# Batch 0's first kv products ahead of the second transposes, and two x products of batches 1 and 2 moved, in an attention-and-GEGLU kernel

## Chip, cores and metric

One core of a Trainium2 chip. The metric is the device time of one execution in microseconds (us), median of several runs. The profiled span is about 1.8 us shorter than the time of the same run and is used for places within the kernel.

## The reference

```python
q_s = softmax(q, axis=-1)              # over the head dimension, 64
k_s = softmax(k, axis=2)               # over the sequence, 576
kv  = einsum('bhsd,bhse->bhde', k_s, v)
x   = einsum('bhsd,bhde->bhse', q_s, kv)    # 8 batches, 8 heads
x   = x.transpose(0, 2, 1, 3).reshape(4608, 512)
out = (gelu(x @ w_gate) * (x @ w_val)) @ w_out   # d_ff = 1536
```

Of the kernel before, what the change touches and what calls it, by code (L numbers as in the profile page):

```python
# [18 lines left out]
def kernel(  # L19
# [17 lines left out]
    NFI = F // P  # L37
# [56 lines left out]
    wg_sb = wpool.tile([P, HP, F], f16, name="wg_sb")  # L94
    wv_sb = wpool.tile([P, HP, F], f16, name="wv_sb")
# [28 lines left out]
    def copy_on(eng, dst, src):  # L124
        if eng == "pool":
            nc.gpsimd.tensor_copy(out=dst, in_=src)  # L126
        elif eng == "act":
            nc.scalar.copy(out=dst, in_=src)  # L128
        else:
            nc.vector.tensor_copy(out=dst, in_=src)  # L130

    def cast_w(nm, c, eng="pool"):
        dst = (wg_sb if nm == "wg" else wv_sb)[:, :, WCH[c]:WCH[c + 1]]
        copy_on(eng, dst, wst[(nm, c)])
# [18 lines left out]
    def cast_v(b, h0, h1, eng="pool"):  # L153
        if eng == "pool" and h1 - h0 > 2:
            for h in range(h0, h1, 2):
                cast_v(b, h, h + 2)
            return
        copy_on(eng, v16_b[b % 2][:, :, h0:h1, 0:D].rearrange("p n h d -> p h n d"),
                tiles[("v", b)][:, h0:h1, :].rearrange("p h (n d) -> p h n d", d=D))
# [44 lines left out]
    st = {}  # L204

    def kv_mm(b, g, j):
        if (b, "pskv", g) not in st:
            pool, tag = (ps_big, "mm") if (b, g) == (0, 1) else (ps_att, "att")
            st[(b, "pskv", g)] = pool.tile([P, 2, 2 * VW], f32, name="pskv", tag=tag)
        hp = 2 * g + j  # L210
        for n in range(NC):
            nc.tensor.matmul(  # L212
                st[(b, "pskv", g)][:, j, :], ek_b[b % 2][:, n, hp * P:(hp + 1) * P],
                v16_b[b % 2][:, n, 2 * hp:2 * hp + 2, 0:VW],
                start=(n == 0), stop=(n == NC - 1))

    def kv_norm(b, g):
        pskv = st[(b, "pskv", g)]
        rck = att.tile([P, 2], f32, name="rck", tag="rck")
        nc.vector.reciprocal(out=rck, in_=pskv[:, :, D])  # L220
        for j in range(2):
            kv_sb = att.tile([P, 2, D], f16, name="kv_sb", tag="kv", bufs=12)
            nc.vector.scalar_tensor_tensor(  # L223
                out=kv_sb,
                in0=pskv[:, j, :].rearrange("p (h e) -> p h e", e=VW)[:, :, 0:D],
                scalar=rck[:, j:j + 1], in1=mask, op0=ALU.mult, op1=ALU.mult)
            st[(b, "kv", 2 * g + j)] = kv_sb
# [6 lines left out]
    def get_eqt(b):  # L234
        if (b, "eqt") not in st:
            st[(b, "eqt")] = att.tile([P, HP * 4 * NC * 32], f16, name="eqt", tag="eqt")[
                :, 0:HP * S].rearrange("p (h t) -> p h t", h=HP)
        return st[(b, "eqt")]

    def unit_t(b, g, eng="dve"):  # L240
        eqt = get_eqt(b)
        pst = ps_att.tile([P, 2, MAIN], f16, name="pst", tag="att")
        for j in range(2):
            hp = 2 * g + j
            for n in range(NM):
                nc.tensor.transpose(  # L246
                    pst[:, j, n * P:(n + 1) * P],
                    eq_b[b % 2][:, n + 1, hp * P:(hp + 1) * P], ident)
        st["evac_t"] = lambda eng: copy_on(eng, eqt[:, 2 * g:2 * g + 2, 0:MAIN], pst)
        if eng:  # L250
            st["evac_t"](eng)
# [66 lines left out]
    def warm_pe(n):  # L318
        ps = pswarm
        for _ in range(n):  # L320
            nc.tensor.matmul(ps, ident, warm, start=True, stop=True)  # L321
# [5 lines left out]
    def mm_gv(ps, w, xt, fi, cis):  # L327
        for ci in cis:
            nc.tensor.matmul(ps, w[:, ci, fi * P:(fi + 1) * P], xt[:, ci, :],  # L329
                             start=(ci == 0), stop=(ci == HP - 1))  # L330

    def gate(psg, psv):
        gl = ffn.tile([P, 512], f32, name="gl", tag="gl")
        nc.scalar.activation(out=gl, in_=psg, func=ACTF.Gelu)  # L334
        ht = htp.tile([P, 512], f16, name="ht", tag="ht")
        nc.vector.scalar_tensor_tensor(  # L336
            out=ht, in0=psv, scalar=_H_SCALE, in1=gl, op0=ALU.mult, op1=ALU.mult)
        return ht
# [5 lines left out]
        mm_gv(psv, wv_sb, xt, fi, range(HP))  # L344
        return gate(psg, psv)

    def ffn_first(xt, after):

        ps = []
        for fi in range(len(after)):  # L350
            psg = ps_big.tile([P, 512], f32, name="psg", tag="mm")
            mm_gv(psg, wg_sb, xt, fi, range(0, 2))
            psv = ps_big.tile([P, 512], f32, name="psv", tag="mm")
            mm_gv(psv, wv_sb, xt, fi, range(0, 2))
            ps.append((psg, psv))
            for f in after[fi]:
                f()
        for fi, (psg, psv) in enumerate(ps):
            mm_gv(psg, wg_sb, xt, fi, [2])
            mm_gv(psv, wv_sb, xt, fi, [2])  # L360
        hts = []
        for fi, (psg, psv) in enumerate(ps):
            mm_gv(psg, wg_sb, xt, fi, [3])
            mm_gv(psv, wv_sb, xt, fi, [3])
            hts.append(gate(psg, psv))
        return hts

    def ffn_first0(xt, xs):

        ps = {}  # L370
        for fi in range(2):
            for nm in ("g", "v"):
                ps[(nm, fi)] = ps_big.tile([P, 512], f32, name="ps" + nm, tag="mm")

        def go(fi, cis):
            for ci in cis:
                mm_gv(ps[("g", fi)], wg_sb, xt, fi, [ci])
                mm_gv(ps[("v", fi)], wv_sb, xt, fi, [ci])

        go(0, (0, 1))  # L380
        xs()
        go(1, (0, 1))
        go(0, (2,))
        go(1, (2,))
        hts = []
        for fi in range(2):
            go(fi, (3,))
            hts.append(gate(ps[("g", fi)], ps[("v", fi)]))
        return hts
# [85 lines left out]
    evac_t0 = st["evac_t"]  # L475
    norm_pair(0, 1, 1, ("dve", "pool"))
    evac_t0("dve")
    warm_pe(9)
    unit_t(0, 1, None)
    cast_v(0, 0, 2, "dve")  # L480
    cast_v(0, 2, 4, "act")
    cast_v(0, 6, 8, "dve")
    cast_v(0, 4, 6, "act")
    st["evac_t"]("act")
    for h0 in (0, 4):
        load(k, "k", 1, h0, h0 + 4, 0)
        load(v, "v", 1, h0, h0 + 4, 0)
    load_batch(2, ((q, "q"), (k, "k")))
    nc.sync.dma_start(out=q0r, in_=q[0].rearrange("h (m n) d -> m h (n d)", n=NT)[:, :, 0:D])
    warm_pe(1)  # L490
    kv_mm(0, 0, 0)
    kv_mm(0, 0, 1)
    kv_norm(0, 0)
    kv_mm(0, 1, 1)
    cast_w("wg", 0, "pool")
    cast_w("wv", 0, "pool")
# [12 lines left out]
    FI, NS = 0, 1  # L509
    plan = {}  # L510

    def at(b, kind, i, *fns):
        plan.setdefault((b, kind, i), []).extend(fns)

    L = lambda f, *a: (lambda: f(*a))
# [7 lines left out]
    at(0, NS, 6, L(norm, 1, 3))  # L523
    at(0, NS, 17, L(unit_x, 1, 0, "act", True), L(unit_x, 1, 1, "act", True))
    at(0, NS, 7, L(preload, ACTF.Gelu))
    first1 = [[L(unit_kv, 1, 1), L(unit_t, 1, 1)], [L(unit_x, 1, 2, "act")],
              [L(unit_x, 1, 3, "dve")]]

    def x_upper():
        unit_x(0, 2, "dve")  # L530
# [13 lines left out]
    at(1, NS, 1, L(unit_x, 2, 0, "dve"))  # L544
    at(1, NS, 12, L(unit_kv, 2, 1))
    at(1, NS, 2, L(unit_x, 2, 1, "dve"), L(unit_x, 2, 2, "dve"))
    at(1, NS, 3, L(unit_x, 2, 3, "act"))
    at(2, FI, 0, L(unit_xrem, 2, "dve"))
    at(2, FI, 7, L(norm_rem0))
    at(3, FI, 8, L(unit_trem, 0))  # L550
# [32 lines left out]
    def ride(b, kind, i):  # L583
        for fn in plan.get((b, kind, i), []):
            fn()

    for b in order:
        xt = get_xt(b) if b < B else xtr
        hts = []
        fi0 = 0  # L590
        if b < 2:
            hts = ffn_first0(xt, x_upper) if b == 0 else ffn_first(xt, first1)
            fi0 = len(hts)
            ride(b, FI, fi0 - 1)
        for fi in range(fi0, NFI):
            hts.append(ffn_fi(xt, fi))
            ride(b, FI, fi)
        if b == 0:
            psys = []
            for ns in range(4):  # L600
                psys.append(ps_big.tile([P, C], f32, name="psy", tag="mm"))
                mm_out(psys[ns], hts, ns, range(0, NFI // 2))
                ride(b, NS, ns)
            for ns in range(4):
                cut = 9 if ns == 3 else NFI
                mm_out(psys[ns], hts, ns, range(NFI // 2, cut))
                ride(b, NS, 14 + ns)
                mm_out(psys[ns], hts, ns, range(cut, NFI))
                evac(b, ns, psys[ns], "act" if ns == 3 else "dve")
                ride(b, NS, 4 + ns)  # L610
        else:
            for ns in range(4):
                if b == order[-1] and ns == 3:
                    last_rows(b, hts, ns)
                    break
                psy = ps_big.tile([P, C], f32, name="psy", tag="mm")
                mm_out(psy, hts, ns, range(NFI // 2))
                ride(b, NS, 10 + ns)
                mm_out(psy, hts, ns, range(NFI // 2, NFI))
                evac(b, ns, psy)  # L620
                ride(b, NS, ns)
# [30 lines left out]
```

## The kernel before: what the change touches

The work is cut by batch. For a batch, q is normalised (`norm`), transposed 128x128 at a time into a PSUM tile `pst` (`unit_t`) that is then copied to `eqt` (the evacuation); `kv_mm` gives `pskv` for two head pairs, `kv_norm` scales it into `kv_sb`; `unit_x` multiplies both into `psx`, which is cast into a row `xt[:, hp]` (four rows per batch, one for each head pair). A gate tile (`fi`) adds four such rows (`ci`) into `psg` and into `psv`. `psxr` is the x product of the rows that are left over when 576 is cut into 128s. `psy` is the output product. The schedule is written by hand: TensorE takes its instructions in the order of this code.

```python
# start, batch 0
    norm_pair(0, 1, 1, ("dve", "pool"))
    evac_t0("dve")
    warm_pe(9)                     # matmuls without use, to fill the wait
    unit_t(0, 1, None)             # second transposes
    cast_v(0, 0, 2, "dve"); cast_v(0, 2, 4, "act")
    cast_v(0, 6, 8, "dve"); cast_v(0, 4, 6, "act")
    st["evac_t"]("act")            # ScalarE copies them out of PSUM
    ...                            # (loads cut)
    warm_pe(1)
    kv_mm(0, 0, 0); kv_mm(0, 0, 1)
    kv_norm(0, 0)
    kv_mm(0, 1, 1)
    ...
    unit_x(0, 0, "act", True)      # then kv_mm(0, 1, 0), unit_x(0, 1), first gate matmul
# batch 1's first three gate tiles
    def ffn_first(xt, after):
        for fi in range(len(after)):
            psg = ...; mm_gv(psg, wg_sb, xt, fi, range(0, 2))
            psv = ...; mm_gv(psv, wv_sb, xt, fi, range(0, 2))
            for f in after[fi]: f()
        ...                        # then row 2 of all three, then row 3
    first1 = [[L(unit_kv, 1, 1), L(unit_t, 1, 1)], [L(unit_x, 1, 2, "act")],
              [L(unit_x, 1, 3, "dve")]]
# what rides behind what; NS 10..13: amid an output tile, NS 0..3: behind it
    at(1, FI, 7, L(exp, "k", 2, 0, 4), L(cast_v, 2, 0, H))
    at(1, FI, 11, L(load_batch, 3), ..., L(cast_v, 3, 0, H))
    at(1, NS, 3, L(unit_x, 2, 3, "act"))
    ...                            # batch 0's last output tile:
    cut = 9 if ns == 3 else NFI    # the x products of batch 1 go behind the cut
```

The softmax here doesn't subtract the row's maximum and nothing guards it: scores larger than these inputs give would overflow.

## Time and profile before

| | before |
|---|---|
| time, median of the first 3 runs | 320.91 us (320.80 to 320.92) |
| span of the profiled run | 319.1 us |
| TensorE busy | 312.4 us, 98% |
| VectorE, ScalarE, GpSimd busy | 193.8, 140.6, 45.2 us |
| TensorE's waits in its own list | six short ones, all before 88 us |

How the gaps between matmuls are counted (from start to start, with a step of 0.216 us at 512 columns), and the lines themselves, are in the prediction.

### The profile page before, as it was taken

How to read it: one execution, taken by the hardware profiler on the slowest of the kernel's cores; microseconds unless marked ns; L12 is line 12 of the kernel's file. 1: busy time of each engine (PE TensorE's matmuls, PEld its weight loads, DVE VectorE, ACT ScalarE, POOL GpSimd, SP SyncE). 2: the span in 40 equal slices, each digit the busy share in tenths (PEclk: the TensorE clock that was granted, in tenths of full speed). 3: DMA queues.
4: the chain of work that ended last, by engine and by line, in shares of the span. 5: the costliest groups of instructions: out<-in, count | busy, mean ns of one | idle time of the engine just before them, and what ended most of it. 6: DMA issues, size and time to landing. Idle time of an engine off the chain costs nothing.

```text
span 319.1 us, 4464 instructions
## 1 busy us (share of the span) xinstructions
PE 312.4 (98%) x1644; PEld 149.0 (47%) x1644; DVE 193.8 (61%) x340; ACT 140.6 (44%) x180; POOL 45.2 (14%) x59
## 2 busy tenths in 40 slices
PE   8899999999999999999999999999999999999995
PEld 3444454445445444544444444444444444444443
DVE  3844386598889479846794679457952444233331
ACT  3763564988342663246433743284221233103300
POOL 2657551330003000110003000300000000000000
PEclk9999999999999999999999999999999999999999
DMA  7999999940196117811492139303011110040002
GB/s 230 372 383 396 399 386 387 390 153 0 66 312 237 50 66 230 312 52 66 143 373 77 42 120 380 107 15 131 1 53 32 66 68 0 18 107 9 0 35 99
DMA packets 42342, 50.76 MB, mean 159 GB/s; under 512 B 3408, under 2 KB 38096, under 8 KB 42320
## 3 DMA queue, kind: packets, MB, share of 16 engines
q1 hardware_dynamic: 40592, 48.84, 44.2%
q10 hardware_dynamic: 1728, 1.64, 1.6%
q8 instruction: 13, 0.21, 0.3%
q14 instruction: 9, 0.07, 0.1%
HBM read 37.75 MB, written 9.44 MB: 148 GB/s over the span
## 4 chain that ended last, share of the span: by engine, by line
PE 93%; ACT 2%; DMA 2%; DVE 1%; issue 1%; POOL 0%; ACTq 0%; POOLq 0%
PE psg L329 29%; PE psy L396 28%; PE psv L329 28%; PE pskv L212 3%; PE psx L305 2%; DMA qt<-in_q_dram 2%; PE psl L417 1%; PE pst L246 1%; PE pswarm L321 1%; ACT eq L148 1%; POOL eq L184 0%; ACT L334 0%; ACT L148 0%; DVE rq L175 0%; DVE kv_sb L223 0%
## 5 line engine op out<-in xcount | busy, mean ns | idle before, releaser
L334 ACT ACTIVATE gl<-psg 128x512 f32<-128x512 f32 x108 | 63.9, 598 | 127.4 <-PE psg L329 125.7
L336 DVE SCALAR_TENSOR_TENSOR ht<-psv,gl 128x512 f16<-128x512 f32 x108 | 72.9, 682 | 64.0 <-PE psv L329 62.4
L329 PE MATMUL psg<-xt,wg_sb 128*128 128x512 f16 x384 | 100.8, 379 | 0.3 <-ACT xt L128 0.2
L329 PE MATMUL psv<-xt,wv_sb 128*128 128x512 f16 x384 | 100.5, 379 | 0.0
L396 PE MATMUL psy<-wo_sb,ht 128*128 128x512 f16 x420 | 95.5, 379 | 0.0
L329 PEld LDWEIGHTS <-wv_sb 128*128 128x128 f16 x432 | 42.3, 98 | 51.8 <-issue 1.3
L329 PEld LDWEIGHTS <-wg_sb 128*128 128x128 f16 x432 | 41.6, 98 | 47.4 <-issue 0.8
L396 PEld LDWEIGHTS <-ht 128*128 128x128 f16 x420 | 40.5, 98 | 47.2 <-DVE ht L336 0.2
L445 DVE TENSOR_SCALAR yo<-psy 128x512 f32<-128x512 f32 x30 | 20.7, 689 | 31.1 <-PE psy L396 31.0
L126 POOL CAST v<-vt 128x640 f16<-128x640 f32 x26 | 19.0, 773 | 139.1 <-DMA vt<-in_v_dram 121.8
L165 DVE TENSOR_REDUCE rq<-eq 128x10 f32<-128x640 f16 x28 | 22.7, 812 | 4.9 <-ACT eq L148 4.5
L184 DVE TENSOR_TENSOR eq<-eq,rrq 128x640 f16<-128x640 f16 (+1 forms) x29 | 23.5, 809 | 0.3
L148 ACT ACTIVATE ek<-kt 128x1280 f16<-128x1280 f32 (+1 forms) x11 | 19.1, 1746 | 3.3 <-DMA kt<-in_k_dram 3.3
L148 ACT ACTIVATE eq<-qt 128x2560 f16<-128x2560 f32 (+2 forms) x10 | 18.4, 1863 | 2.4 <-DMA qt<-in_q_dram 2.3
L271 DVE STREAM_TRANSPOSE et<-eq 128x640 f16<-128x640 f16 x20 | 16.9, 845 | 0.7
L128 ACT CAST xt<-psx 128x512 f16<-128x512 f32 x17 | 9.3, 587 | 14.6 <-PE psx L305 14.6
L329 PE MATMUL psg<-xtr,wg_sb 128*128 128x512 f16 x48 | 12.3, 379 | 0.0
L329 PE MATMUL psv<-xtr,wv_sb 128*128 128x512 f16 x48 | 12.3, 379 | 0.0
L321 PE MATMUL pswarm<-warm,ident 128*128 128x512 f16 x40 | 10.8, 431 | 1.4 <-POOL ident masks.py:199 1.4
L212 PEld LDWEIGHTS <-ek 128*128 128x128 f16 x160 | 10.5, 97 | 3.3
L212 PE MATMUL pskv<-v,ek 128*128 128x130 f16 x160 | 11.8, 220 | 0.0
L130 DVE CAST xt<-psx 128x512 f16<-128x512 f32 x15 | 9.7, 682 | 2.4 <-PE psx L305 2.4
(61 smaller groups left out, 129.6 us busy)
## 6 DMA issues: line engine op xcount, KB each, us to landing
out_dram<-yo SPq DMA_DIRECT2D x14, 512.0 KB, 3.5
kt<-in_k_dram SPq DMA_DIRECT2D x7, 640.0 KB, 7.8
vt<-in_v_dram SPq DMA_DIRECT2D x7, 640.0 KB, 8.1
qt<-in_q_dram SPq DMA_DIRECT2D x7, 640.0 KB, 5.8
qt<-in_q_dram SPq DMA_DIRECT2D x8, 512.0 KB, 6.5
eqt<-et SPq DMA_DIRECT2D x80, 40.0 KB, 1.9
wost<-in_moe_w_out_dram SPq DMA_DIRECT2D x6, 512.0 KB, 7.9
kt<-in_k_dram SPq DMA_DIRECT2D x6, 512.0 KB, 8.0
```

The costliest lines, as they stand in the source:

```text
L126: nc.gpsimd.tensor_copy(out=dst, in_=src)
L148: nc.scalar.activation(out=dst[:, n0:NC, h0 * D:h1 * D].rearrange("p n (h d) -> p h n d", d=D), in_=tiles[(nm, b)][:, h0:h1, n0 * D:NC * D ...
L165: nc.vector.reduce_sum(rq, e, axis=mybir.AxisListType.X)
L184: (nc.gpsimd if eng == "pool" else nc.vector).tensor_tensor(out=e, in0=e, in1=rrq.unsqueeze(-1).to_broadcast((P, n, 2, D)), op=ALU.mult)
L212: nc.tensor.matmul(st[(b, "pskv", g)][:, j, :], ek_b[b % 2][:, n, hp * P:(hp + 1) * P], v16_b[b % 2][:, n, 2 * hp:2 * hp + 2, 0:VW], start ...
L271: nc.vector.transpose(out=et[:, :, hp].rearrange("p c (n i) -> p n c i", i=32), in_=eq_b[b % 2][:, :, hp * P:(hp + 1) * P].rearrange("p n ...
L321: nc.tensor.matmul(ps, ident, warm, start=True, stop=True)
L329: nc.tensor.matmul(ps, w[:, ci, fi * P:(fi + 1) * P], xt[:, ci, :], start=(ci == 0), stop=(ci == HP - 1))
L334: nc.scalar.activation(out=gl, in_=psg, func=ACTF.Gelu)
L336: nc.vector.scalar_tensor_tensor(out=ht, in0=psv, scalar=_H_SCALE, in1=gl, op0=ALU.mult, op1=ALU.mult)
L396: nc.tensor.matmul(psy, hts[fi][:, ns * P:(ns + 1) * P], wo_sb[:, fi, :], start=(fi == 0), stop=(fi == NFI - 1))
L445: nc.vector.tensor_scalar(out=yo, in0=psy, scalar1=1.0 / _H_SCALE, scalar2=None, op0=ALU.mult)
```

## The change

The intent: take what nothing needs yet out of the way of batch 0's first kv product, and fill three gaps later on. I call the pieces A (start), B (batch 1's first gate tiles with the cut) and C (batch 2's last x product).

```diff
# A
-    warm_pe(9)
-    unit_t(0, 1, None)
+    warm_pe(11)
     cast_v(0, 0, 2, "dve")          # (three more casts cut)
-    st["evac_t"]("act")
-    warm_pe(1)
     kv_mm(0, 0, 0)
     kv_mm(0, 0, 1)
     kv_norm(0, 0)
+    unit_t(0, 1, "dve")
     kv_mm(0, 1, 1)
# B, in ffn_first
+            if fi == 0:
+                for ci in range(2):
+                    mm_gv(psg, wg_sb, xt, fi, [ci])
+                    mm_gv(psv, wv_sb, xt, fi, [ci])
+            else:
+                mm_gv(psg, wg_sb, xt, fi, range(0, 2))
+                for f in between[fi]: f()
+                mm_gv(psv, wv_sb, xt, fi, range(0, 2))
-    first1 = [[L(unit_kv, 1, 1), L(unit_t, 1, 1)], [L(unit_x, 1, 2, "act")],
-              [L(unit_x, 1, 3, "dve")]]
+    first1 = ([[L(unit_kv, 1, 1), L(unit_t, 1, 1)], [], [L(unit_x, 1, 3, "dve")]],
+              [[], [], [L(unit_x, 1, 2, "act")]])
-                cut = 9 if ns == 3 else NFI
+                cut = 10 if ns == 3 else NFI
# C
-    at(1, NS, 3, L(unit_x, 2, 3, "act"))
+    at(1, NS, 13, L(unit_x, 2, 3, "act"))
```

More of the change, by code (lines that the diff above doesn't have):

```diff
@@ L345, in ffn_fi, with ffn_first @@
         return gate(psg, psv)
-    def ffn_first(xt, after):
+    def ffn_first(xt, after, between):
         ps = []
@@ L351, in ffn_first @@
             psg = ps_big.tile([P, 512], f32, name="psg", tag="mm")
-            mm_gv(psg, wg_sb, xt, fi, range(0, 2))
             psv = ps_big.tile([P, 512], f32, name="psv", tag="mm")
-            mm_gv(psv, wv_sb, xt, fi, range(0, 2))
+            if fi == 0:
[4 more added lines that the diff above has]
+                mm_gv(psg, wg_sb, xt, fi, range(0, 2))
+                for f in between[fi]:
+                    f()
+                mm_gv(psv, wv_sb, xt, fi, range(0, 2))
             ps.append((psg, psv))
@@ L591 @@
         if b < 2:
-            hts = ffn_first0(xt, x_upper) if b == 0 else ffn_first(xt, first1)
+            hts = ffn_first0(xt, x_upper) if b == 0 else ffn_first(xt, *first1)
             fi0 = len(hts)
```

## The prediction

> **What bounds the kernel now.** I read the page first, then TensorE's waits, then the chain that ended last in the three stretches that the diff touches, and the timeline there for the true starts.
>
> ```profile
> PE 312.4 (98%) x1644; PEld 149.0 (47%) x1644; DVE 193.8 (61%) x340; ACT 140.6 (44%) x180; POOL 45.2 (14%) x59
> ...
> PE 93%; ACT 2%; DMA 2%; DVE 1%; issue 1%; POOL 0%; ACTq 0%; POOLq 0%
> ```
>
> TensorE is the bound: 98% busy and 93% of the chain. The change removes almost no matmul (one warm one more, eleven instead of nine plus one), so it can win only from the gaps between matmuls. TensorE's list of waits is short; after 88 us it has none, so all that can be had lies before.
>
> ```profile
> PE psx L305 <- DVE kv_sb L223: 0.4, 1, 0.4
> PE psx L305 <- DVE eqt L130: 0.2, 1, 0.2
> PE psg L329 <- ACT xt L128: 0.2, 1, 0.2
> ```
>
> These are too small to take at their word: a matmul of 512 columns is drawn 0.38 us long, but the next may start 0.216 us after it (36 of them fill 7.93 us: 35 steps and one 0.38). A gap under 0.16 us is hidden behind the drawn end. I therefore count gaps from start to start.
>
> The start of the kernel, in the chain (start us, us, what):
>
> ```profile
> 13.32 0.45 PE pst L246 x8
> 13.77 0.22 PE pswarm L321
> 13.98 0.59 PE pskv L212 x10
> 14.57 0.03 issue
> 14.60 0.18 DVE rck L220
> 14.78 0.03 issue
> 14.80 0.36 DVE kv_sb L223
> 15.16 0.05 issue
> 15.21 0.40 PE psx L305
> 15.61 0.02 issue
> 15.64 0.59 ACT xt L128
> ```
>
> The second transposes (pst x8) and a warm matmul stand on the chain ahead of the first kv product (pskv), though nothing in the chain needs them there: what follows pskv is VectorE's normalisation, the x product and its cast, then the first gate matmul at 16.27.
>
> Batch 1's first gate tiles, in the same view:
>
> ```profile
> 48.40 0.65 PE psx L305 x2
> ...
> 49.69 0.22 PE psg L329
> ...
> 49.95 0.38 PE psg L329
> ...
> 52.18 0.61 DVE eqt L130
> ...
> 52.83 0.38 PE psx L305
> ...
> 54.28 0.21 PE psg L329
> ```
>
> The x products wait for kv_sb (48.40), the second psg matmul for the second row of x (49.95), and the third x product for VectorE's evacuation of the transposes (52.83). The end of batch 1:
>
> ```profile
> 86.59 0.65 PE psg L329 x3
> ...
> 87.26 0.38 PE psg L329
> ```
>
> Three of batch 2's first four psg matmuls run at once; the fourth waits for the last row of x, whose product ran only at 86.21.
>
> **What the Trainium skill says.** "TensorE: Matmul & The Clock Gate", section "Wait — 56ns, not 53.3ns?", gives 215.7 ns from start to start at 512 columns with a warm array; the 0.2157 us above agrees. "VectorE: DVE Perf Modes", section "The perf-mode tier table", lets a copy with a PSUM operand reach at most 2x. The trace agrees: VectorE copies 1024 f16 from PSUM in 0.68 us, as long as 512 f32. "ScalarE: Activation LUTs", section "What ACT_TABLE_LOAD costs", gives 186 ns + 0.833 ns per element; for 1024 that is 1.04 us, and the trace has 1.00 for the evacuation that the change takes from ScalarE. "SBUF — State Buffer", section "Who interferes with whom", says that a VectorE instruction with at most one SBUF input and outside the two-port modes doesn't contend with GpSimd. The moved evacuation reads PSUM, so GpSimd's weight casts shouldn't suffer; in the trace the first evacuation, already on VectorE at 12.08, lies beside a GpSimd multiply of 1.49 us, against 1.48 for the one without it.
>
> **Part A, the start.** Before, by the timeline, nine warm matmuls begin at 11.21, the transposes at 13.16, one warm matmul at 13.60, kv at 13.82. After, eleven warm ones: 11.21 + 11 x 0.2157 = 13.58, and kv starts there, as v's first heads are cast on VectorE by about 13.4 and ScalarE's (heads 2, 3) by about 13.45. Kv starts 0.24 earlier. Ten kv matmuls (0.58) end at 14.16; VectorE (idle 0.78 before rck) starts rck at 14.36 and the first kv_sb is ready for the x product at 15.21 - 0.24 = 14.97. TensorE meanwhile does the eight transposes (0.44, to 14.60) and five kv matmuls (0.29, to 14.89): the transposes fit in a wait of about half a microsecond that exists today (kv_sb 0.4 in the list). Then the casts and the gate matmul follow 0.24 earlier, at 16.03. VectorE's evacuation runs from the end of kv_sb, 15.17, to 15.85; the second kv normalisation starts at about 15.9, as today (15.92), and gives its first kv_sb near 16.45, needed at 17.20 - 0.24 = 16.96. It fits. **A: 0.24 us.** The weights must be cast that much earlier: the tightest is the fourth piece of w_val, cast by 23.74 and needed at 24.54 - 0.24 = 24.30.
>
> **Part B, batch 1's first gate tiles**, in the clock of before. Kv ends at 47.58. With the cut at 10, four psy matmuls follow instead of three: 47.58 + 4 x 0.2157 = 48.44, so the first x product starts at 48.44 in place of waiting from 48.23 to 48.40; the second starts at 48.67 as today, when its kv_sb is ready. Two psy matmuls end at 49.31. From an x product's start to the matmul that reads its ScalarE cast takes 16.27 - 15.21 = 1.06 us, so psg's first starts at 49.50, psv's first at 49.72; the second row comes at 49.95 + 0.04 = 49.99: psg, psv, end 50.42. Before it was 50.59: 0.17 won. Kv and transposes follow to 51.44, psg and psv of the second tile to 52.31, psg of the third to 52.74. The evacuation moves with kv (VectorE idled 0.33 before rck), is ready at 52.83 - 0.17 = 52.66, and the x product starts at 52.74 with no wait. Psv's two matmuls and the fourth x product follow, to 53.61; but the third row needs 1.06 us and comes at 53.80. So psg's third ci starts at 53.80 instead of 54.12. The 0.36 us gap in front of the x product is traded for one of 0.19 behind it. The fourth row (product at 53.39, VectorE cast 0.69) is there near 54.5, needed at 53.80 + 6 x 0.2157 = 55.09. **B: 54.12 - 53.80 = 0.32 us**, which includes the 0.17.
>
> **Part C, the last x product of batch 2** goes from 86.21 to the middle of the last psy tile, 83.62 + 6 x 0.2157 = 84.91. Its PSUM buffer is free when VectorE's first of two casts (from 84.00, 1.28 both) ends, near 84.7; ScalarE sat idle for 5.31 us. The row is then ready before 86.2. The gap was 87.48 - (86.42 + 4 x 0.2157) = 0.20, and it closes. **C: 0.20 us.**
>
> Sum: 0.24 + 0.32 + 0.20 = 0.76, and 320.91 - 0.76 = 320.15 us, if all that follows moves along.
>
> **Rivals.** (1) ScalarE as a new bound between 58 and 64 us: its chain gelu 58.00, table load, exp of 2.34, table load at 62.26, gelu 63.56 makes TensorE wait for a PSUM buffer until 64.21, 0.26 after the previous tile's 63.95. If that chain had a clock of its own, A and B would be eaten and only C left: 320.7. For it: it is on the chain. Against it: its first gelu waits for TensorE (ScalarE idle 0.59) and q's load is long in, so it moves along. (2) The evacuation on VectorE delays the second kv normalisation by over half a microsecond, or batch 1's data come too late from DMA (ScalarE waited for k at 42.87): A would be lost, 320.4. The slack of half a microsecond, and of over 1 us for kv at 47.00, speak against it. (3) The early x product in C waits for its buffer (0.2 us of slack only): the gap is moved, not closed, 320.35. (4) The casts are quicker than 1.06 us after a product, and B's leftover gaps of 0.19 close as well: 319.9.
>
> **Range and chances.** Terms add with little interplay; I allow about a third of the sum either way and 0.1 between sessions (the three runs differ by 0.12): 319.8 to 320.5. Two per cent would be 6.4 us, more than all of TensorE's gaps after the first load, and there is no step that could lose as much. So within 2% is nearly certain.
>
> **What would show it.** In the changed kernel: kv at 13.58, first gate matmul near 16.03; from there to batch 1's first psg matmul on the third row 37.53 us (54.12 - 16.27 = 37.85 before, less B's 0.32); the third x product without a wait but a new wait on ScalarE's xt behind it; no gap at batch 2's fourth psg. I am wrong if the gain of 54 us is gone by 64 us, if a weight cast holds TensorE near 24 us, or if the gap in C reappears in front of the x product.

## The result, and the profile after

The changed kernel takes 320.26 us (320.11 to 320.37, 6 runs) against 321.06 (320.80 to 321.46, 6 runs) for the kernel before in the same rounds. The ratio is 0.9973, interval 0.9960 to 0.9986: a gain of 0.27%. A ratio is the mean time of one kernel's runs over that of the other's of the same rounds, so not quite the ratio of the medians quoted. The predicted 320.15 lies 0.11 from the measured median.

The page of the changed kernel, busy times and chain by engine:

```profile
PE 312.0 (98%) x1645; PEld 148.9 (47%) x1645; DVE 194.7 (61%) x341; ACT 139.7 (44%) x179; POOL 44.8 (14%) x59
...
PE 88%; DMA 4%; ACT 3%; DVE 2%; issue 1%; POOL 0%; ACTq 0%; DVEq 0%; POOLq 0%
```

TensorE's work is the same, but its share of the chain fell from 93% to 88%: the chain now leaves TensorE in places (told below). From TensorE's waits (total, times, longest):

```profile
PE pst L246 <- DVE eq L184: 0.7, 1, 0.7
...
PE psg L329 <- ACT xt L128: 0.2, 1, 0.2
```

The waits of psx for kv_sb and for eqt have gone; the 0.7 is ahead of the first transposes, where the data of the first load arrive, and differs from run to run.

The chain at the start (start us, us, what):

```profile
11.30 2.37 PE pswarm L321 x11
13.67 0.57 PE pskv L212 x10
14.24 0.45 PE pst L246 x8
14.69 0.29 PE pskv L212 x5
14.98 0.32 PE psx L305
```

Kv now stands in front of the transposes, and the transposes fill what was the wait for kv_sb. TensorE's timeline amid batch 1's first gate tiles:

```profile
52.41 0.38 PE L305 MATMUL psx<-eqt,kv_sb 128*128 128x512 f16 x1
...
53.47 0.38 PE L329 MATMUL psg<-xt,wg_sb 128*128 128x512 f16 x1
```

The third x product (52.41) runs without a wait; the third row's psg (53.47) starts 1.06 us after it, as worked out. And in the chain at the end of batch 1:

```profile
84.62 0.22 PE psx L305
84.83 1.29 PE psy L403 x6
86.13 0.86 PE psg L329 x4
```

All four psg matmuls in one go: C's gap has closed. Measured from one mark to the next on TensorE:

| stretch | before | after | won |
|---|---|---|---|
| first matmul of the group of 9 or 11 warm ones to first kv | 13.82 - 11.21 = 2.61 | 13.51 - 11.13 = 2.38 | 0.23 |
| first kv to first gate matmul | 2.45 | 2.45 | 0 |
| first gate matmul to batch 1's psg on the third row | 37.85 | 37.51 | 0.34 |
| that to the psg that waits for ScalarE's gelu (64.21, 63.55) | 10.09 | 10.08 | 0 |
| third row's psg to batch 1's first psy matmul | 73.83 - 54.12 = 19.71 | 73.37 - 53.47 = 19.90 | -0.19 |
| first psy matmul to batch 2's psxr | 88.34 - 73.83 = 14.51 | 87.69 - 73.37 = 14.32 | 0.19 |
| that psxr to the end of the span | 230.76 | 230.76 | 0 |

So A, B and C came as predicted, and 0.19 us was lost between 64 and 73 us, where the prediction has nothing. The timeline shows it; before:

```profile
68.40 0.83 DVE L184 TENSOR_TENSOR eq<-eq,rrq 128x640 f16<-128x640 f16 x1
...
68.81 3.58 POOL L126 CAST v<-vt 128x640 f16<-128x640 f32 x4 [7.53 <-PE psg L329]
...
70.83 0.98 DVE L184 TENSOR_TENSOR eq<-eq,rrq 128x640 f16<-128x640 f16 x1
...
71.60 0.67 PE L246 MATMUL pst<-ident,eq 128*128 128x128 f16 x8
```

and after:

```profile
67.74 0.82 DVE L184 TENSOR_TENSOR eq<-eq,rrq 128x640 f16<-128x640 f16 x1
...
68.62 3.31 POOL L126 CAST v<-vt 128x640 f16<-128x640 f32 x4 [7.52 <-DMA vt<-in_v_dram]
...
70.18 1.17 DVE L184 TENSOR_TENSOR eq<-eq,rrq 128x640 f16<-128x640 f16 x1
...
70.94 0.86 PE L246 MATMUL pst<-ident,eq 128*128 128x128 f16 x8
71.41 0.23 PEld L246 LDWEIGHTS <-eq 128*128 128x128 f16 x4 [0.25 <-DVE eq L184]
```

VectorE's third and fourth multiplies normalise batch 2's last two head pairs; the second transposes need the fourth. It takes 0.82 us undisturbed, 0.98 before and 1.17 after, and what it takes longer TensorE waits: the eight transposes fill 0.86 instead of 0.67, with 0.25 of waiting in front of the fifth's weights. Beside it GpSimd casts batch 3's v in four pieces. These start when the DMA has brought v: at 68.81 and 68.62, each 0.15 us after v's second load landed (68.67 and 68.48 in the traces; the release by PE named in the first had long been done). So v came 0.19 us earlier, while VectorE's work came 0.65 us earlier. This is also one place where the chain leaves TensorE: from 63.5 to 71.4 us it runs through VectorE's normalisation of batch 2, which in the kernel before it did not touch. The other is not to be believed: from 50.9 to 57.9 us the chain is put down to an output store that is said to release ScalarE's table load at 57.96. That load starts 0.02 us after the gelu ahead of it ends (57.94), as in the kernel before (58.62 after 58.60), so it waited for no store.

The Trainium skill, page "SBUF — State Buffer", section "Who interferes with whom", says that a VectorE instruction with two SBUF inputs contends with a GpSimd instruction that reads SBUF, and that the order of issue decides which of them is blocked. The lines agree: the multiply that started behind a piece of the cast took 0.98 and 1.17 us. I had cited that section for the moved evacuation (one PSUM input, no contention; it took 0.68 us at 15.01 beside casts of 0.62, so that holds) and not asked which other instructions my shift would bring together.

### The profile page after: what moved, and what is told of

Read it like the earlier page. It is cut to its first block, busy times and chain, and to the rows that moved or that the text cites. A ratio compares the mean times of both kernels' runs of the same rounds, so it can differ in the third digit from the quotient of the medians.

```text
span 318.5 us, 4464 instructions
## 1 busy us (share of the span) xinstructions
PE 312.0 (98%) x1645; PEld 148.9 (47%) x1645; DVE 194.7 (61%) x341; ACT 139.7 (44%) x179; POOL 44.8 (14%) x59
## 4 chain that ended last, share of the span: by engine, by line
PE 88%; DMA 4%; ACT 3%; DVE 2%; issue 1%; POOL 0%; ACTq 0%; DVEq 0%; POOLq 0%
PE psy L403 28%; PE psg L329 26%; PE psv L329 26%; PE pskv L212 3%; DMA out_dram<-yo 2%; PE psx L305 2%; DMA qt<-in_q_dram 2%; PE psl L424 1%; PE pswarm L321 1%; DVE rq L165 1%; DVE ht L336 1%; ACT eq L148 1%; PE pst L246 1%; ACT xt L128 1%; POOL eq L184 0%
```

## The experiments

**Theory 1**: gains move along, and 0.19 is a chance of one profile. **Theory 2**: GpSimd's cast of v has a clock of its own (the DMA's) and takes back what comes early. Four kernels on one chip first (before there: 320.89 us, 9 runs). For several the interval of the ratio reaches 1, so that only the marks in the profile show what they won.

**1. A alone** (the diff's part A on the kernel before).

> The kernel before with part A alone (eleven warm matmuls, kv ahead of the second transposes, their evacuation on VectorE). From the first transpose's start to the first kv matmul 3.43 us in place of 3.66, to the first gate matmul 5.88 in place of 6.11: 0.23 us won at 16 us under every theory. Theory 1 (the gain moves along): it is still there at batch 1's first psy matmul (73.83 before, so near 73.6) and in the time, 0.997 to 0.9995, or 0.2 us. Theory 2 (batch 3's v cast on GpSimd, started by its DMA at about 68.7, holds the shared path against VectorE's last multiply for batch 2, at 70.83 in the kernel before): the multiply comes 0.2 earlier, takes about 1.2 us in place of 0.98, and TensorE's second transposes of batch 2 wait about 0.25; the gain after 74 us is 0.05 or less.

Measured: 320.58 us, ratio 0.9984 (0.9971 to 0.9998). The first transposes began late in this profile (TensorE's warm matmuls were slower), so the marks from there do not compare; from the warm matmuls to kv it is 13.56 - 11.19 = 2.37 us against 2.61, kv to gate 2.46. So 0.24 won. But from the third row to the first psy 19.70, and the fourth multiply took 0.97, not 1.2: nothing was lost. Theory 2 in this form is wrong for this kernel.

**2. B alone** (part B).

> The kernel before with part B alone (rows of x in batch 1's first gate tile, the cut at 10, the third x product inside the third tile). From the first gate matmul of batch 0 to batch 1's first psg on the third row 37.52 us in place of 37.85: 0.33 won at 54 us. Theory 1: 0.33 is still there after 74 us. Theory 2: the multiply before batch 2's second transposes takes 1.2 to 1.35 us, TensorE waits there, and between 0 and 0.15 is left after 74 us.

Measured: 320.91 us, ratio 0.9992 (0.9980 to 1.0005). Gate to third row 37.51: the 0.34 is there in the profile. Again 19.70 and 0.97: nothing lost. A second miss for theory 2 as I had put it.

**3. C alone** (part C).

> The kernel before with part C alone (batch 2's last x product before the second half of the last psy tile). Both theories: from batch 1's first psy matmul to the first psxr of batch 2 14.32 us in place of 14.51, so 0.19 won, nothing changed before 84 us, and as nothing behind it has a clock of its own, 0.2 us in the time (ratio near 0.9994).

Measured: 320.75 us, ratio 0.9994 (0.9981 to 1.0006), 14.32 us from the first psy to psxr: 0.19 won, as both said.

**4. The changed kernel with batch 3's v later.**

```diff
-    at(1, FI, 11, L(load_batch, 3), ..., L(cast_v, 3, 0, H))
+    at(1, FI, 11, L(load_batch, 3, ((q, "q"), (k, "k"))), ...)
-    at(1, NS, 1, L(unit_x, 2, 0, "dve"))
+    at(1, NS, 1, L(load_batch, 3, ((v, "v"),)), L(cast_v, 3, 0, H), L(unit_x, 2, 0, "dve"))
```

> The changed kernel with batch 3's v load and cast put behind the second output store of batch 1 (about 81 us in place of 61), so that GpSimd is idle while VectorE multiplies for batch 2. Theory 2: the last multiply falls from 1.17 to 0.82 us, the wait in front of the fifth of batch 2's second transposes goes from 0.25 to 0, the first psy matmul comes 0.25 us earlier against the third row's psg (19.65 us after it in place of 19.90), and the time falls by 0.2 to 0.3 below the changed kernel, so a ratio near 0.9965 against the kernel before. Theory 1: the multiply stays at 1.1 us or more, and the time is that of the changed kernel. Against both: the later load could hold a later store or batch 3's kv (about 97 us); then a new wait stands there.

Measured: 319.95 us, ratio 0.9969 (0.9956 to 0.9981). GpSimd casts v at 87 us, and at the fourth multiply the timeline has

```profile
70.49 0.83 DVE L184 TENSOR_TENSOR eq<-eq,rrq 128x640 f16<-128x640 f16 x1
```

with 19.64 us from the third row to psy, and from psxr to the end 230.77 as against 230.76. The cast of v is what lengthens the multiply, then. The load moved along with it, but in the changed kernel it had landed at 68.48, 1.7 us before the multiply began. In the time the step from 0.9973 to 0.9969 lies inside the intervals.

Why then did A and B alone not lose? Their profiles show the cast's first piece starting at 68.65 and 68.42, *inside* VectorE's third multiply (68.14 + 0.83, 67.88 + 0.83): it is held up until that ends (0.89 and 0.86 us instead of 0.72), and so GpSimd falls into step with VectorE. In the changed kernel the third multiply ended at 68.56 and the cast began at 68.62: no hold, no step. That is **theory 2, refined**, and runs 5 to 7 test it (before on the chip of runs 5 to 8: 320.91, 9 runs).

**5. The changed kernel again**, unedited.

> The changed kernel once more, on the chip of the next three. The refined theory: GpSimd's four casts of batch 3's v begin when the DMA is in, near 68.6 us, which does not move with TensorE. If that falls inside VectorE's third multiply for batch 2, the first cast is held to the multiply's end, and the fourth multiply then meets the third cast at a fixed phase and takes 0.97 us (before, and all three single parts). If the third multiply has ended by then, the casts run free, and the fourth multiply takes 1.17 (up to 1.35). The changed kernel is 0.65 us early there and stands at the edge: so again 1.17 and 19.90 us from the third row's psg to the first psy matmul, or, where DMA is in 0.1 earlier, 0.97 and 19.70. Ratio to before 0.997 to 0.998.

Measured: 320.18 us, ratio 0.9974 (0.9961 to 0.9986). Here v came 0.4 us earlier:

```profile
67.71 0.83 DVE L184 TENSOR_TENSOR eq<-eq,rrq 128x640 f16<-128x640 f16 x1
...
68.21 3.50 POOL L126 CAST v<-vt 128x640 f16<-128x640 f32 x4 [7.49 <-DMA vt<-in_v_dram]
...
70.15 0.98 DVE L184 TENSOR_TENSOR eq<-eq,rrq 128x640 f16<-128x640 f16 x1
...
70.92 0.67 PE L246 MATMUL pst<-ident,eq 128*128 128x128 f16 x8
```

The cast starts inside the third multiply, the fourth takes 0.98, and 19.71 us pass from the third row to psy: nothing lost, with the same kernel. So the 0.19 is no fixed price of the change; it comes and goes with the arrival of v.

**6. The changed kernel with ten warm matmuls** (`warm_pe(11)` to `warm_pe(10)`).

> The changed kernel with ten warm matmuls in place of eleven. v's first heads are cast by 13.33 to 13.40, so the first kv matmul can start up to 0.18 us earlier (13.51 in the changed kernel). By the refined theory the fourth multiply then comes at about 70.0, just after the third cast's start, takes 1.3 to 1.4 us, and the 0.15 won at 16 us is lost at 71 us: 20.0 to 20.1 us from the third row to the first psy matmul and a time within 0.1 of the changed kernel. If gains simply add: 0.15 less than the changed kernel.

Measured: 319.96 us, ratio 0.9966 (0.9953 to 0.9980). Kv at 13.34, and

```profile
67.57 0.83 DVE L184 TENSOR_TENSOR eq<-eq,rrq 128x640 f16<-128x640 f16 x1
...
68.55 3.31 POOL L126 CAST v<-vt 128x640 f16<-128x640 f32 x4 [7.52 <-DMA vt<-in_v_dram]
...
70.00 1.28 DVE L184 TENSOR_TENSOR eq<-eq,rrq 128x640 f16<-128x640 f16 x1
...
71.34 0.40 PE L246 MATMUL pst<-ident,eq 128*128 128x128 f16 x4 [0.18 <-DVE eq L184]
```

The cast starts 0.16 us after the third multiply's end, the fourth takes 1.28, and 20.01 us pass to psy: 0.30 lost. The profile is as the refined theory had it (the multiply a little under its 1.3 to 1.4). The time is not: it was to lie within 0.1 of the changed kernel's, and its median lies 0.22 below. That suggests that not every run loses; the intervals overlap, so this stays open.

Four profiles follow one rule, found after these runs. The third piece of the cast began 0.42 us (before), 0.22 (after), 0.41 (again) and 0.12 (ten warm) ahead of the fourth multiply, and the multiply took 0.15, 0.35, 0.15 and 0.45 more than its 0.83: in each case 0.57 in all. It looks as if the multiply waits until the piece under way is 0.57 us old; why 0.57 and not the piece's full 0.72 is not shown. Over all fourteen profiles, the multiply took 0.97 or 0.98 us in the nine in which the cast's first piece was held, 1.17 and 1.28 in the two in which it was not, and 0.82 or 0.83 in the three without the cast.

**7. Ten warm matmuls and v late** (6 and 4 together).

> The changed kernel with ten warm matmuls and with batch 3's v load and cast behind the second store of batch 1. With GpSimd idle there, nothing is lost at 71 us: multiply 0.83, 19.64 us from the third row to the first psy matmul; first kv matmul 0.15 earlier than in the changed kernel. 0.4 us below the changed kernel, ratio near 0.996 against the kernel before.

Measured: 319.98 us, ratio 0.9968 (0.9956 to 0.9981). Multiply 0.83 and 19.65, as expected; but the first transposes' second half started only at 11.24, against 10.90 in the changed kernel, and kv at 13.73. The time missed: 0.20 below the changed kernel's in place of 0.4, and not below that of ten warm matmuls alone (319.96), so the time does not show what the late v is worth. In the fourteen profiles the first load lands between 6.44 and 6.87 us, a spread as large as what I was looking for.

**8. The kernel before, with two warm matmuls fewer** (`warm_pe(9)` to 8, `warm_pe(1)` dropped; order and evacuation as before). A rival for A: is it the order, or only the count of matmuls in TensorE's queue ahead of kv?

> The kernel before with eight warm matmuls and none, in place of nine and one; transposes still ahead of kv, evacuated by ScalarE. Rival to the order: part A's 0.23 is only what leaves TensorE's queue ahead of kv (eight transposes and one warm matmul, 0.66, less two warm ones, 0.43). If so, dropping two warm matmuls without any reordering wins as much or more: 0.40 us from first warm matmul after the first transposes to the gate (limited by v's casts at about 13.35), first kv matmul near 13.40, and a ratio near 0.9988. If the order is needed (evacuation on ScalarE or the kv wait holding), the gate stays within 0.1 of 16.27.

Measured: 320.65 us, ratio 0.9989 (0.9977 to 1.0002). The timeline:

```profile
11.24 1.89 PE L321 MATMUL pswarm<-warm,ident 128*128 128x512 f16 x8
12.97 0.61 PE L246 MATMUL pst<-ident,eq 128*128 128x128 f16 x8
13.52 1.02 PE L212 MATMUL pskv<-v,ek 128*128 128x130 f16 x15
14.90 0.39 PE L305 MATMUL psx<-eqt,kv_sb 128*128 128x512 f16 x1 [0.36 <-DVE kv_sb L223]
```

From the warm matmuls to kv 13.52 - 11.24 = 2.28 us, against 2.61 before and 2.38 after; the gate starts at 15.97, after at 15.96. So the order isn't needed for A. What counts is what is queued ahead of kv: eight transposes and ten warm matmuls take 0.44 + 2.16 = 2.60, eleven warm ones 2.37, transposes and eight warm ones 2.17, to which a wait of 0.11 for v's cast is added. With transposes first TensorE still waits 0.36 for kv_sb, and from kv to the gate it takes 2.45 us all the same.

Then B in parts, on a third chip (before there: 321.07, 9 runs). The first three are one look each, for the profile.

**9. Order by rows alone** (third x product and cut as before).

> Of part B only the order by rows of x in batch 1's first gate tile; the cut stays at 9 and the third x product behind the second tile. From batch 1's first kv to its second kv: 3.59 us before, 3.41 in the changed kernel. If the rows alone are the cause: 3.39 to 3.42, since with the cut at 9 the first row's matmuls run without a wait (at 49.53 of the kernel before) and the second row's at 49.96. If rows and cut are needed together: 3.5. From batch 0's first gate matmul to the third row's psg 37.85 less the same.

Measured: 320.75 us in one run. Kv to kv 50.41 - 47.02 = 3.39, gate to third row 37.65: 0.20 won by the rows alone.

**10. The cut at 10 alone.**

> Of part B only the cut at 10. If my sum in the prediction is right that the chain of x product, cast and gate matmul bounds here, the second row still comes at 49.99 and three matmuls follow it: 3.60 to 3.64 us from batch 1's first kv to its second, so nothing is won. If the wait of 0.17 in front of the first x product was a true loss, 3.42.

Measured: 321.53 us in one run. Kv to kv 50.63 - 47.01 = 3.62, gate to third row 37.90: nothing won, 0.03 to 0.05 lost.

**11. The third x product inside the third tile, alone.**

> Of part B only the third x product inside the third tile. kv to kv 3.59 as before. From batch 0's first gate matmul to the third row's psg: the x product starts at 52.90 (before's clock) in place of 52.83, and the row is there 1.06 later, 53.96 in place of 54.12: 37.69 us. If it gave all of B's 0.34, 37.51.

Measured: 320.71 us in one run. Gate to third row 37.68: 0.17 won, and 0.20 + 0.17 - 0.03 is B's 0.34.

**12. All that helped: the changed kernel with ten warm matmuls, v late and the cut back at 9.**

> The changed kernel with ten warm matmuls, batch 3's v late and the cut back at 9. kv to kv 3.39 to 3.42, as in the changed kernel, so the cut is worth nothing; from the third row to the first psy matmul 19.64; ratio to before 0.996 to 0.997, as the same version with the cut at 10 (0.9968).

Measured: 319.87 us (319.73 to 320.24, 5 runs) against 321.07, ratio 0.9963 (0.9949 to 0.9976), span 318.0. Kv to kv 3.38, multiply 0.82, 19.65. It beats the kernel before clearly. Against the changed kernel (0.9973, 0.9974 on other chips) the profile has it ahead at every mark, but the intervals overlap, and they did not run side by side.

## Why the prediction was right

- **What bounds it**: right. TensorE runs 1645 matmuls after and 1644 before, and the marks find the gain where the gaps were. (Its busy time fell all the same, from 312.4 to 312.0 us: a gap shorter than 0.16 us is drawn as busy.)
- **A, 0.24**: 0.23 in the changed kernel, 0.24 alone. The steps held: kv waited for no cast (it started 2.38 us after the first of eleven warm ones, and 11 x 0.2157 is 2.37), the transposes filled the wait for kv_sb, VectorE's second kv normalisation came in time (at 15.61; I had 15.9, but its instructions overlap by some 0.09 each and the run's data came 0.08 early). But the reason is the shorter queue, not the order (experiment 8), which the sum of A said without drawing the conclusion.
- **B, 0.32**: 0.34. The 1.06 us from an x product to the matmul that reads its cast held at 52.41 to 53.47. The text lumped rows and cut together for 0.17; apart they are 0.20 and -0.03. The leftover gap of 0.19 in front of the third row is there.
- **C, 0.20**: 0.19. The buffer came free in time.
- **Rival 1** (ScalarE with a clock of its own between 58 and 64 us): wrong, 10.09 and 10.08 us over that stretch. **Rivals 2 to 4**: not seen; A's gain was there at 16 us, C's gap gone, B's leftover gap still there.
- **"If all that follows moves along"**: the one step that didn't always hold. GpSimd's cast of batch 3's v follows the DMA and not TensorE, and in the profiled run of the changed kernel it took back 0.19 us; in another profiled run of the same kernel it took nothing. The prediction did look for an engine with a clock of its own, but for ScalarE, between 58 and 64 us; the loss came after 64 us, and its signs of being wrong do not cover it.
- **The sum**: 0.76 predicted. In the first profile 0.23 + 0.34 + 0.19 - 0.19 = 0.57, and the kernel started 0.08 earlier by the arrival of its first data: 0.65, and the spans differ by 0.6. In the repeat the marks give 0.24 + 0.34 + 0.19 = 0.77, without the loss. The medians differ by 0.80 and 0.73. The interval of the time, 0.14% to 0.40%, is some 0.45 to 1.3 us, so it can't tell these apart; the marks in the profile can. That the median came within 0.11 us is thus in part luck: the sizes of A, B and C were right, but whether 0.19 is lost behind them depends on when v arrives, which the prediction did not ask.

## What to carry to other kernels

Where one engine is busy all the time, count gaps from start to start and follow a gain past the stretch it was made in: work that a DMA's arrival starts need not move along (the cast of v came 0.19 us earlier, all around it 0.65), and a shift brings new neighbours together. Before reordering work ahead of a wait, ask whether dropping filler does the same. Gains of a few tenths of a microsecond are read from marks within the profile, as the spread of arrivals from run to run is as large (0.4 us for the first load).

## What the Trainium skill lacked or had wrong

- "SBUF — State Buffer", "Who interferes with whom": right on which instructions contend, but without sizes for such a pair. Here a 0.83 us multiply beside casts of 0.72 us each took up to 1.28, and its start offset plus its extra time was 0.57 us in four profiles, as if it got going some 0.15 us before the cast's drawn end (an estimate: 0.72 - 0.57); a piece held by a multiply ended 0.58 us after it.
- The same section doesn't say that a hold can bring two engines into step and so make later collisions cheaper (0.97 or 0.98 where the cast's first piece was held, 1.17 and 1.28 where it wasn't).
- "TensorE: Matmul & The Clock Gate": the step of 215.7 ns agrees. No page says that a gap below some 0.16 us between such matmuls leaves no trace as idle time (drawn 0.38, step 0.216); "Perfetto Trace Analysis" has the drawn end as an estimate only.
- No page gives the time from one matmul's start to the next that reads its result through a ScalarE cast of 512 columns: 1.06 us here, of which 0.59 is the cast.
